# Sixty constant products ahead of the last batch's first tokens, and a change of halves between ScalarE and VectorE

## The chip, the core and the metric

The kernel runs on one core of a Trainium2 chip. The metric is the device time of one execution in microseconds (us), lower is better; the number compared is the median of several runs. The profile is one execution, taken by the hardware profiler, with times from the start of its span.

## What is computed

Attention with a memory term, then a mixture of experts that sends each token to one expert. Cut to what matters here:

```python
B, H, S, D = 4, 8, 576, 64                      # attention
scores = where(causal, -1e9, q @ k.T / sqrt(D))
local = softmax(scores) @ v
out = g * mem_out + (1 - g) * local             # g per head, mem_out from phi(q), M_prev, z_prev
x = out.transpose(0, 2, 1, 3).reshape(2304, 512)

logits = x @ w_gate + modality_bias[modality_id]    # 8 experts
e = argmax(logits); gate_w = softmax(logits)[e]
out[n] = gate_w[n] * (relu(x[n] @ w1[e]) @ w2[e])   # w1 512x1024, w2 1024x512 per expert
```

## The kernel before, in words

Everything is float32; a product of two float32 matrices is made of three faster ones, from a high part and the rest of each operand ("h" and "l" in the names of tiles).

**Order.** A planner (`Plan`) takes every operation with an engine, a planned length, the keys that it reads and writes (`r`, `w`) and a priority, simulates the engines and writes the instructions out in the order in which its simulation starts them. Each engine runs its own list in order. The keys and the planned lengths only set this order. What an engine waits for on the chip is decided afterwards, from the tiles that each instruction really reads and writes.

**Attention** fills the first 310 us or so, head by head. `av` multiplies the probabilities by `vhl`, whose 128 columns are 64 of the high part of v and 64 of its rest, so that a PSUM bank holds the result of the high part on partitions 0 to 63 and that of the rest on 64 to 127. The two have to be added. For half of the heads (`d % 4 < 2`) ScalarE copies both and GpSimd adds them; for the others ScalarE copies one to the tile `avt` (L738) and VectorE adds the other from PSUM (L740), into partitions 0 to 63 of `ot` for an even head and 64 to 127 for an odd one. Each such head has two copies and two additions (128 and 448 columns), 32 of each in all.

**Experts.** After each batch of 576 tokens the gate and `route` write tables of token numbers by expert, and a slot of 256 rows of the fullest expert is worked on at once: `fetch` loads the slot's rows of the tables (SyncE, L1009), `merge` turns them into the tile `ids` (VectorE, L999 and L1000), and GpSimd gathers the tokens from `x_dram` into `xg` (L1016). `slot` then transposes them on TensorE (L1042), ScalarE and VectorE make `xh` and `xl` (L1050, L1052), and TensorE makes 8 groups of 12 products with w1 (L1064), one PSUM bank for each group; ScalarE (relu, L1073, `hh`) and VectorE (the rest, L1075, `hlo`) empty each bank. Products with w2 follow (L1086), 24 for each tile of tokens. Slots 0 to 2 belong to the first three batches. Slot 3 (two tiles of 128 tokens) and slot 4 (two of 96) are the first that can hold tokens of the last batch. All TensorE's results share 8 banks (`pa_90` to `pa_97`). Meanwhile the weights of the second expert are loaded (SyncE, L978) into a ring of four tiles `raw`, rounded by ScalarE (L985) and the rest taken by VectorE (L989), which frees the ring's tile; its last eight pieces are `w2h` and `w2l`.

At the program's start TensorE multiplies a tile of ones by itself 90 times (`warm`, L501).

Of the kernel before, what the change touches and what calls it, by code (L numbers as in the profile page):

```python
# [12 lines left out]
AF = mybir.ActivationFunctionType  # L13
ALU = mybir.AluOpType
# [198 lines left out]
def kernel(  # L213
# [15 lines left out]
    nc = tc.nc  # L229
# [4 lines left out]
    P = 128  # L234
# [13 lines left out]
    EARLY = 3  # L248
# [35 lines left out]
    NH = B * H  # L284
    NAVP = 2
    NRELU = 4
    INPLACE = (0,)
    NWARM = 90
    VHI = "POOL"
    WLO = "POOL"  # L290
    NDBL = 0
# [205 lines left out]
    def warm():  # L497

        t = Slot()
        for i in range(NWARM):  # L500
            g.op("PE", 56, lambda: nc.tensor.matmul(t.ap[:, 0:P], lhsT=ones, rhs=ones, start=True, stop=True),  # L501
                 r=[t] if i else ["ones"], w=[] if i else [t], alloc=None if i else t, prio=("warm", 9))

    def load_t(nm, src, p, prio):
        b, h0 = divmod(p * 2, H)
# [201 lines left out]
    def av(d, prio):  # L707
        p, hh = divmod(d, 2)
        vt = vhl[p % 2]
        ta, tb = Slot(), Slot()  # L710

        def e(src, first, part):
            for kb in range(NB):
                if kb == 0 and part == 0:
                    nc.tensor.matmul(ta.ap[:, 0:P], lhsT=vt[:, 0, hh], rhs=src[:, PTO[0]:PTO[0] + P],
                                     start=first, stop=not first)
                if part == 1:
                    q0 = max(P, kb * P)
                    s0 = PTO[kb] + q0 - kb * P
                    nc.tensor.matmul(tb.ap[:, q0 - P:S - P], lhsT=vt[:, kb, hh], rhs=src[:, s0:s0 + S - q0],  # L720
                                     start=(first and kb == 0), stop=(not first and kb == NB - 1))

        vk = [(x, p % 2, c) for x in ("vh", "vl") for c in (0, 4)]
        for part, (t, du, ky) in enumerate(((ta, 155, "AB"), (tb, 780, "ABCD"))):
            g.op("PE", du, lambda part=part: e(pth[0], True, part), r=vk + [("ph_", 0, x) for x in ky], w=[t], alloc=t,
                 prio=prio, act=0.88)
            g.op("PE", du, lambda part=part: e(ptl[0], False, part), r=vk + [("pl_", 0, x) for x in ky], w=[t], prio=prio,
                 act=0.88)
        o_, a_ = ot[p % 2][64 * hh:64 * hh + 64], avt[0][64 * hh:64 * hh + 64]
        for part, (t, a, z) in enumerate(((ta, 0, P), (tb, P, S))):  # L730
            n, ko = z - a, ("ot", p % 2, hh, part)
            if d % 4 < NAVP:
                g.op("ACT", act_ns(n), lambda t=t, a=a, z=z, n=n: nc.scalar.activation(
                    out=o_[:, a:z], in_=t.ap[0:64, 0:n], func=AF.Copy), r=[t], w=[ko], prio=prio)
                g.op("ACT", act_ns(n), lambda t=t, a=a, z=z, n=n: nc.scalar.activation(  # L735
                    out=a_[:, a:z], in_=t.ap[64:P, 0:n], func=AF.Copy), r=[t], w=[("avt", part)], prio=prio)
            else:
                g.op("ACT", act_ns(n), lambda t=t, a=a, z=z, n=n: nc.scalar.activation(  # L738
                    out=avt[0][0:64, a:z], in_=t.ap[64:P, 0:n], func=AF.Copy), r=[t], w=[("avt", part)], prio=prio)
                g.op("DVE", dve_ns(n), lambda t=t, a=a, z=z, n=n: nc.vector.tensor_tensor(  # L740
                    out=o_[:, a:z], in0=t.ap[0:64, 0:n], in1=avt[0][0:64, a:z], op=ALU.add),
                     r=[t, ("avt", part)], w=[ko], prio=prio)
        if d % 4 < NAVP:
            g.op("POOL", 1420, lambda: nc.gpsimd.tensor_tensor(out=o_, in0=o_, in1=a_, op=ALU.add),
                 r=[("avt", 0), ("avt", 1)], w=[("ot", p % 2, hh, 0), ("ot", p % 2, hh, 1)], prio=prio)
# [286 lines left out]
    def slot(g, u, w, nt, prio, m=P):  # L1032

        i4, i2, n_ = u % 4, pick(u), nt * m
        id_, nc_ = ids[i4], 2 if nt < 3 else 1
        for y in range(KC // nc_):
            ps_ = Slot()

            def e1(y=y, ps_=ps_):
                for c in range(nc_):  # L1040
                    for t in range(nt):
                        nc.tensor.transpose(ps_.ap[:, c * n_ + t * m:c * n_ + (t + 1) * m],  # L1042
                                            xg[i2][0:m, t, (nc_ * y + c) * P:(nc_ * y + c + 1) * P], ident[0:m, 0:m])

            def pv(ps_=ps_):
                return ps_.ap[:, 0:nc_ * n_].rearrange("p (c n) -> p c n", n=n_)

            cs = slice(nc_ * y, nc_ * y + nc_)
            g.op("PE", 107 * nt * nc_, e1, r=[("xg", i2, t) for t in range(nt)], w=[ps_], alloc=ps_, prio=prio)
            g.op("ACT", act_ns(nc_ * n_), lambda cs=cs, pv=pv: nc.scalar.activation(  # L1050
                out=xh[i2][:, cs, 0:n_], in_=pv(), func=AF.Copy), r=[ps_], w=[("xh", i2, nc_ * y // 2)], prio=prio)
            g.op("DVE", dve_ns(nc_ * n_), lambda cs=cs, pv=pv: nc.vector.tensor_tensor(  # L1052
                out=xl[i2][:, cs, 0:n_], in0=pv(), in1=xh[i2][:, cs, 0:n_].bitcast(F32), op=ALU.subtract),
                 r=[ps_, ("xh", i2, nc_ * y // 2)], w=[("xl", i2, nc_ * y // 2)], prio=prio)
        xk = [(x, i2, y) for x in ("xh", "xl") for y in range(2)]
        for f in range(KF):
            hp = Slot()

            def e2(f=f, hp=hp):
                n = 0  # L1060
                w1h, w1l = wt[w][0:2]
                for c in range(KC):
                    for a, x_ in ((w1h, xh[i2]), (w1h, xl[i2]), (w1l, xh[i2])):
                        nc.tensor.matmul(hp.ap[:, 0:n_], lhsT=a[:, c, f * P:(f + 1) * P], rhs=x_[:, c, 0:n_],  # L1064
                                         start=(n == 0), stop=(n == 3 * KC - 1))
                        n += 1

            g.op("PE", 12 * pe_ns(n_) + 25, e2, r=xk + [k_ for c in range(KC) for k_ in wkeys(w, c)],
                 w=[hp], alloc=hp, prio=prio)
            for i, (a, z) in enumerate(((0, min(n_, 2 * P)), (2 * P, n_))):  # L1070
                if a >= z:
                    continue
                g.op("ACT", act_ns(z - a), lambda f=f, hp=hp, i=i, a=a, z=z: nc.scalar.activation(  # L1073
                    out=hh[i][:, f, 0:z - a], in_=hp.ap[:, a:z], func=AF.Relu), r=[hp], w=[("hh", i, f)], prio=prio)
                g.op("DVE", dve_ns(z - a), lambda f=f, hp=hp, i=i, a=a, z=z: nc.vector.scalar_tensor_tensor(  # L1075
                    out=hlo[i][:, f, 0:z - a], in0=hp.ap[:, a:z], scalar=0.0, in1=hh[i][:, f, 0:z - a].bitcast(F32),
                    op0=ALU.max, op1=ALU.subtract), r=[hp, ("hh", i, f)], w=[("hl", i, f)], prio=prio)
        for t in range(nt):
            op, hi, ts = Slot(), t // 2, slice(t % 2 * m, (t % 2 + 1) * m)
            for y in range(4):  # L1080
                def e3(y=y, op=op, hi=hi, ts=ts):
                    n = 0
                    w2h, w2l = wt[w][2:4]
                    for f in range(2 * y, 2 * y + 2):
                        for a, w_ in ((hh[hi], w2h), (hh[hi], w2l), (hlo[hi], w2h)):
                            nc.tensor.matmul(op.ap[0:m], lhsT=a[:, f, ts], rhs=w_[:, f],  # L1086
                                             start=(y == 0 and n == 0), stop=(y == 3 and n == 5))
                            n += 1

                g.op("PE", 6 * pe_ns(512), e3, r=[(x, hi, f) for x in ("hh", "hl") for f in range(2 * y, 2 * y + 2)] +  # L1090
                     wkeys(w, KC + y), w=[op], alloc=op if y == 0 else None, prio=prio)
            oi = 0 if u < EARLY else next_osb()
            g.op("ACT", act_ns(512, True, 1), lambda t=t, op=op, oi=oi: nc.scalar.activation(  # L1093
                out=osb[oi][0:m], in_=op.ap[0:m], func=AF.Copy, scale=id_[0:m, t, 1:2].bitcast(F32)),
                 r=[op, ("ids", i4)], w=[("osb", oi)], prio=prio)
            store(u, t, m, oi, prio)
# [228 lines left out]
    o = 0  # L1325
    for x, (nt, m) in enumerate(NST0):
        fetch(g, u, start(EARLY, o), nt, ["swap"], ("f1", NH + 2 * x), m=m)
        slot(g, u, 0, nt, ("e1", NH + 2 * x), m=m)
        o += nt * m
        u += 1  # L1330
# [91 lines left out]
```

## Time and profile before

| | us |
|---|---|
| time, median of 3 runs (lowest, highest) | 551.55 (549.52, 552.14) |
| profiled execution, its own time | 550.81 |
| its span, first to last instruction | 549.1 |
| TensorE (PE) busy | 497.9, 91% |
| VectorE (DVE) busy | 330.5, 60% |
| ScalarE (ACT) busy | 329.0, 60% |
| GpSimd (POOL) busy | 251.9, 46% |

[...] Shares are means over the whole span; attention and the experts have different limits, and the stretch around the change is read by itself below.

### The profile page before, as it was taken

The page shows a single profiled execution, that of the slowest core. Times are in us where ns is not written, and L with a number is a line of the kernel's source. Part 1 is how long each engine was busy: PE and PEld are TensorE (multiplying, and loading weights), DVE is VectorE, ACT ScalarE, POOL GpSimd, SP SyncE. Part 2 cuts the span into 40 slices and gives each one's busy share as a digit, 9 for nine tenths or more (in the row PEclk, how much of TensorE's full clock was granted, in tenths as well). Part 3 has the DMA queues.
Part 4 walks back from the last instruction along what each step waited for, and adds up shares of the span by engine and source line. Part 5 has one row for each costly group of instructions (what it writes and reads, how often), then busy time and mean ns, then how long its engine had stood idle before and what let it go on. Part 6 is the DMA issues. An engine that isn't in the chain of part 4 may idle for free. (4 is left out here: it accounts for less than half of the span.)

```text
span 549.1 us, 10861 instructions
## 1 busy us (share of the span) xinstructions
PE 497.9 (91%) x3420; PEld 445.1 (81%) x3420; DVE 330.5 (60%) x1066; ACT 329.0 (60%) x923; POOL 251.9 (46%) x257
## 2 busy tenths in 40 slices
PE   8898899987899889979898999769999999999992
PEld 8787888875787778869897898769897987989891
DVE  3788788897798988988878336653315512313010
ACT  4798898986999979979298244333325513222110
POOL 8462984656788768865761062350030004010100
PEclk9799899999899989989899999979999999999997
DMA  5888887988777997953740025474036203000100
GB/s 96 189 206 169 206 201 182 231 189 154 192 176 198 238 189 191 220 164 95 180 110 3 20 61 180 78 233 146 18 96 182 83 19 88 29 19 21 40 0 36
DMA packets 97101, 70.43 MB, mean 128 GB/s; under 512 B 73936, under 2 KB 74320, under 8 KB 97042
## 3 DMA queue, kind: packets, MB, share of 16 engines
q1 hardware_dynamic: 93330, 59.99, 45.2%
q0 software_dynamic: 3712, 9.72, 5.8%
q8 instruction: 28, 0.46, 0.4%
q14 instruction: 31, 0.25, 0.2%
HBM read 32.36 MB, written 10.16 MB: 77 GB/s over the span
## 5 line engine op out<-in xcount | busy, mean ns | idle before, releaser
L675 ACT ACTIVATE P<-P,nm 128x576 f32<-128x576 f32 (+4 forms) x160 | 88.5, 558 | 9.1 <-DVE nm L669 6.0
L1024 POOL DMA_INDIRECT out_dram<-osb,ids x19 | 18.9, 997 | 156.0 <-ACT osb L1093 115.3
L1064 PE MATMUL pa<-xh,w1h 128*128 128x256 f32 (+2 forms) x288 | 84.4, 293 | 2.6 <-ACT xh L1050 2.6
L1064 PE MATMUL pa<-xl,w1h 128*128 128x256 f32 (+2 forms) x288 | 83.4, 290 | 0.5 <-DVE xl L1052 0.3
L1064 PE MATMUL pa<-xh,w1l 128*128 128x256 f32 (+2 forms) x288 | 83.1, 288 | 0.0
L1075 DVE SCALAR_TENSOR_TENSOR hlo<-pa,hh 128x256 fp32r<-128x256 f32 (+1 forms) x72 | 29.8, 416 | 69.8 <-ACT hh L1073 69.7
L703 DVE TENSOR_TENSOR ptl<-pa,pth 128x512 fp32r<-128x512 f32 (+1 forms) x128 | 65.6, 564 | 3.0 <-ACT pth L701 2.4
L1073 ACT ACTIVATE hh<-pa 128x256 fp32r<-128x256 f32 (+1 forms) x80 | 29.0, 367 | 61.1 <-PE pa L1064 54.2
L669 DVE CUSTOM_DVE_ANT_0 P<-pa,maskw 128x320 f32<-128x320 f32 (+3 forms) x160 | 62.2, 427 | 4.2 <-PE pa L657 3.5
L684 PE MATMUL pa<-ident,P 128*128 128x128 f32 x320 | 57.6, 285 | 4.0 <-ACT P L675 3.7
L657 PE MATMUL pa<-ks,qs 128*128 128x192 f32 (+3 forms) x186 | 55.5, 329 | 5.9 <-ACT avt L735 2.9
L1086 PE MATMUL pa<-w2h,hh 128*128 128x512 f32 (+1 forms) x152 | 60.4, 397 | 0.0
L701 ACT ACTIVATE pth<-pa 128x512 fp32r<-128x512 f32 (+1 forms) x128 | 57.0, 511 | 5.0 <-PE pa L684 4.4
L1086 PE MATMUL pa<-w2l,hh 128*128 128x512 f32 (+1 forms) x152 | 59.6, 392 | 0.0
L1064 PEld LDWEIGHTS pa<-xh,w1h 128*128 128x128 f32 x288 | 55.6, 193 | 3.4 <-ACT xh L1050 2.9
L1064 PEld LDWEIGHTS pa<-xl,w1h 128*128 128x128 f32 x288 | 55.6, 193 | 1.2 <-DVE xl L1052 0.9
L1086 PE MATMUL pa<-w2h,hlo 128*128 128x512 f32 (+1 forms) x144 | 56.5, 392 | 0.0
L1064 PEld LDWEIGHTS pa<-xh,w1l 128*128 128x128 f32 x288 | 55.5, 193 | 0.0
L1093 ACT ACTIVATE osb<-pa,ids 128x512 f32<-128x512 f32 (+1 forms) x19 | 13.1, 687 | 68.4 <-PE pa L1086 63.1
L657 PE MATMUL pa<-kls,qs 128*128 128x192 f32 (+3 forms) x186 | 49.2, 295 | 0.4 <-DMA kls<-kl 0.4
L684 PEld LDWEIGHTS pa<-ident,P 128*128 128x128 f32 x320 | 40.4, 147 | 6.3 <-ACT P L675 6.0
L684 PE MATMUL pa<-swp,P 128*128 128x128 f32 x160 | 39.5, 287 | 6.1 <-DVE kl L617 2.5
(234 smaller groups left out, 1198.9 us busy)
## 6 DMA issues: line engine op xcount, KB each, us to landing
ks<-kh SPq DMA_DIRECT2D x62, 144.0 KB, 3.0
kls<-kl SPq DMA_DIRECT2D x62, 144.0 KB, 3.4
raw<-in_moe_w_dram SPq DMA_DIRECT2D x32, 256.0 KB, 3.5
qn<-in_q_dram SPq DMA_DIRECT2D x32, 144.0 KB, 4.3
kn<-in_k_dram SPq DMA_DIRECT2D x32, 144.0 KB, 4.2
qs<-qh SPq DMA_DIRECT2D x31, 144.0 KB, 2.6
qs<-ql SPq DMA_DIRECT2D x31, 144.0 KB, 2.7
vn<-in_v_dram SPq DMA_DIRECT2D x32, 128.0 KB, 3.0
```

The source lines that it names most:

```text
L657: nc.tensor.matmul(t.ap[0:m, o:o + z - x], lhsT=l[:, QS[j]:QE[j]], rhs=r[:, x:z], start=(i == 0), stop=(i == len(terms) - 1))
L669: nc.vector.tensor_tensor_reduce(out=pj[:, x:z], in0=t.ap[0:m, o:o + z - x], in1=mk, scale=-1.0, scalar=nm if x else 3.0e38, op0=ALU.add, ...
L675: g.op("ACT", act_ns(w, False, 2), lambda pj=pj, nm=nm, den=den, w=w: nc.scalar.activation(out=pj[:, 0:w], in_=pj[:, 0:w], func=AF.Exp, sc ...
L684: nc.tensor.transpose(t[:, o:o + P], prow[c % NPB][j][:, kb * P:(kb + 1) * P], swp if j == kb else ident)
L701: g.op("ACT", act_ns(n), lambda t=t, o=o, n=n: nc.scalar.activation(out=hi[:, o:o + n], in_=t.ap[:, 0:n], func=AF.Copy), r=[t], w=[("ph_", ...
L703: g.op("DVE", dve_ns(n), lambda t=t, o=o, n=n: nc.vector.tensor_tensor(out=lo[:, o:o + n], in0=t.ap[:, 0:n], in1=hi[:, o:o + n].bitcast(F3 ...
L1024: g.op("POOL", 1310, lambda: nc.gpsimd.indirect_dma_start(out=out[:, :], out_offset=bass.IndirectOffsetOnAxis(ap=ids[u % 4][0:m, t, 0:1].b ...
L1064: nc.tensor.matmul(hp.ap[:, 0:n_], lhsT=a[:, c, f * P:(f + 1) * P], rhs=x_[:, c, 0:n_], start=(n == 0), stop=(n == 3 * KC - 1))
L1073: g.op("ACT", act_ns(z - a), lambda f=f, hp=hp, i=i, a=a, z=z: nc.scalar.activation(out=hh[i][:, f, 0:z - a], in_=hp.ap[:, a:z], func=AF.R ...
L1075: g.op("DVE", dve_ns(z - a), lambda f=f, hp=hp, i=i, a=a, z=z: nc.vector.scalar_tensor_tensor(out=hlo[i][:, f, 0:z - a], in0=hp.ap[:, a:z] ...
L1086: nc.tensor.matmul(op.ap[0:m], lhsT=a[:, f, ts], rhs=w_[:, f], start=(y == 0 and n == 0), stop=(y == 3 and n == 5))
L1093: g.op("ACT", act_ns(512, True, 1), lambda t=t, op=op, oi=oi: nc.scalar.activation(out=osb[oi][0:m], in_=op.ap[0:m], func=AF.Copy, scale=i ...
```

## The change

Two things. `hot` puts 60 products of the tile of ones into the plan, keyed to the `ids` of slot 3 and ahead of slot 3's transposes. And in `av`, for the heads that VectorE adds, ScalarE now copies partitions 0 to 63 of the bank, and VectorE reads partitions 64 to 127 of the bank beside partitions 0 to 63 of `avt`.

```diff
+    NHOT = 60
+    def hot(u):
+        t = Slot()
+        for i in range(NHOT):
+            g.op("PE", 56, lambda: nc.tensor.matmul(t.ap[:, 0:P], lhsT=ones, rhs=ones, start=True, stop=True),
+                 r=[t] if i else [("ids", u % 4)], w=([] if i else [t]) + ["hot"] * (i == NHOT - 1), alloc=None if i else t,
+                 prio=("f1", NH))
...
-                    out=avt[0][0:64, a:z], in_=t.ap[64:P, 0:n], func=AF.Copy), r=[t], w=[("avt", part)], prio=prio)
+                    out=avt[0][0:64, a:z], in_=t.ap[0:64, 0:n], func=AF.Copy), r=[t], w=[("avt", part)], prio=prio)
-                    out=o_[:, a:z], in0=t.ap[0:64, 0:n], in1=avt[0][0:64, a:z], op=ALU.add),
+                    out=o_[:, a:z], in0=t.ap[64:P, 0:n], in1=avt[0][0:64, a:z], op=ALU.add),
...
-            g.op("PE", 107 * nt * nc_, e1, r=[("xg", i2, t) for t in range(nt)], w=[ps_], alloc=ps_, prio=prio)
+            g.op("PE", 107 * nt * nc_, e1, r=[("xg", i2, t) for t in range(nt)] + (["hot"] if u == EARLY else []), w=[ps_], alloc=ps_, prio=prio)
...
         fetch(g, u, start(EARLY, o), nt, ["swap"], ("f1", NH + 2 * x), m=m)
+        if x == 0:
+            hot(u)
         slot(g, u, 0, nt, ("e1", NH + 2 * x), m=m)
```

Up to the products the order of all engines is the same as before; GpSimd's and SyncE's stay the same to the end. The lines of the changed kernel stand 9 higher in this part (L1064 is L1073 there, L1042 is L1051, L1086 is L1095, L989 is L998, L1075 is L1084, L1052 is L1061).

TensorE before, from the end of slot 2's seventh group. The tile `xh_109` is slot 2's, `xg_4300` and `xh_4296` are slot 3's, `xg_108` is slot 4's; what an instruction waits for stands in brackets.

```order
L1064 MATMUL pa_96<-xh_109,w1l_99 128x256
L1042 MATMUL pa_93<-ident,xg_4300 128x128 [waits DMAHW5_49,DMAHW6_49,DMASW6_49,PE_49]
L1042 MATMUL pa_93<-ident,xg_4300 128x128 [waits DMASW7_49]
...
L1064 MATMUL pa_94<-xh_109,w1h_98 128x256 [waits DVE_49]
...
L1086 MATMUL pa_95<-w2h_100,hh_111 128x512 [waits DVE_49]
...
L1064 MATMUL pa_91<-xh_4296,w1h_98 128x256 [waits DVE_49,Activation_49]
```

After it come five groups of slot 3, the transposes of slot 4, and 18 more products with w2. TensorE in the changed kernel, from the end of slot 2's third group:

```order
L1073 MATMUL pa_95<-xh_109,w1l_99 128x256
L509 LDWEIGHTS ones
L509 MATMUL pa_91<-ones 128x128
...
L1051 MATMUL pa_96<-ident,xg_4300 128x128 [waits DMAHW5_49,DMAHW6_49,DMASW6_49,PE_49]
...
L1073 MATMUL pa_92<-xh_109,w1h_98 128x256 [waits DVE_49]
...
L1051 MATMUL pa_94<-ident,xg_108 128x96 [waits DMASW0_49,DVE_49]
...
L1073 MATMUL pa_91<-xh_4296,w1h_98 128x256 [waits Activation_49]
...
L1095 MATMUL pa_93<-w2h_100,hh_111 128x512 [waits DVE_49]
```

The 60 products stand behind slot 2's third group, with no wait in front of them; its groups 4 and 5 follow, then slot 3's transposes, group 6, slot 4's transposes, four groups of slot 3, groups 7 and 8 of slot 2 (into `pa_93` and `pa_92`), 12 products with w2 into `pa_93`, slot 3's fifth group, 12 more products with w2, and slot 3's sixth group. Before, slot 2's groups 1 to 7 all stood ahead of slot 3's transposes.

VectorE before, from slot 3's `xl` to slot 4's:

```order
L1052 TENSOR_TENSOR xl_4297<-pa_93,xh_4296 128x2x256
L1052 TENSOR_TENSOR xl_4297<-pa_92,xh_4296 128x2x256
L989 TENSOR_TENSOR w2l_4295<-raw_4306,w2h_4294 128x512
L1075 SCALAR_TENSOR_TENSOR hlo_112<-pa_94,hh_111 128x256
L989 TENSOR_TENSOR w2l_4295<-raw_4307,w2h_4294 128x512
L989 TENSOR_TENSOR w2l_4295<-raw_4304,w2h_4294 128x512
L989 TENSOR_TENSOR w2l_4295<-raw_4305,w2h_4294 128x512
L989 TENSOR_TENSOR w2l_4295<-raw_4306,w2h_4294 128x512
L989 TENSOR_TENSOR w2l_4295<-raw_4307,w2h_4294 128x512
L1052 TENSOR_TENSOR xl_110<-pa_92,xh_109 128x2x192
```

VectorE in the changed kernel, the same stretch:

```order
L1061 TENSOR_TENSOR xl_4297<-pa_96,xh_4296 128x2x256
L1061 TENSOR_TENSOR xl_4297<-pa_93,xh_4296 128x2x256
L1084 SCALAR_TENSOR_TENSOR hlo_112<-pa_92,hh_111 128x256
L998 TENSOR_TENSOR w2l_4295<-raw_4307,w2h_4294 128x512
L998 TENSOR_TENSOR w2l_4295<-raw_4304,w2h_4294 128x512
L998 TENSOR_TENSOR w2l_4295<-raw_4305,w2h_4294 128x512
L998 TENSOR_TENSOR w2l_4295<-raw_4306,w2h_4294 128x512
L998 TENSOR_TENSOR w2l_4295<-raw_4307,w2h_4294 128x512
L1084 SCALAR_TENSOR_TENSOR hlo_112<-pa_93,hh_111 128x256
L1084 SCALAR_TENSOR_TENSOR hlo_112<-pa_92,hh_111 128x256
L1061 TENSOR_TENSOR xl_110<-pa_94,xh_109 128x2x192
```

The `hlo` of slot 2's groups 7 and 8 (`pa_93`, `pa_92`) now stand behind the last five pieces of w2. On ScalarE the two relus moved in the same way, behind the last five pieces of `w2h`.

## Rows read from the trace of the kernel before

**Rows 1.** The page's part 2: TensorE's busy tenths in 40 slices of 13.7 us.

```profile
PE   8898899987899889979898999769999999999992
```

**Rows 2.** TensorE by time: start, length, instructions; in brackets idle time before and its releaser.

```profile
353.16 0.28 PE L1064 MATMUL pa<-xh,w1l 128*128 128x256 f32 x1
...
358.60 0.28 PE L1064 MATMUL pa<-xh,w1l 128*128 128x256 f32 x1
362.13 0.45 PE L1042 MATMUL pa<-ident,xg 128*128 128x128 f32 x1 [3.25 <-issue]
364.03 1.75 PE L1042 MATMUL pa<-ident,xg 128*128 128x128 f32 x7 [1.46 <-DMA xg<-x_dram,ids]
365.44 0.56 PE L1064 MATMUL pa<-xh,w1h 128*128 128x256 f32 x1
...
368.14 0.41 PE L1086 MATMUL pa<-w2h,hh 128*128 128x512 f32 x1
...
369.56 0.28 PE L1064 MATMUL pa<-xh,w1h 128*128 128x256 f32 x1
...
376.63 0.82 PE L1042 MATMUL pa<-ident,xg 96*128 96x96 f32 x8
...
377.55 0.40 PE L1086 MATMUL pa<-w2l,hh 128*128 128x512 f32 x1
...
381.52 0.28 PE L1064 MATMUL pa<-xh,w1h 128*128 128x256 f32 x1
```

**Rows 3.** Stretches of 1 us: engines' busy time, then granted clock, DMA share, GB/s.

```profile
361.00:362.00 1.00, 0.00 (x0) 0.00 (x0) 0.83 (x2) 0.95 (x3) 0.70 (x2) 0.66 0.75 146
...
368.00:369.00 1.00, 1.00 (x6) 0.86 (x6) 0.28 (x2) 0.39 (x1) 0.15 (x1) 0.92 0.86 260
```

**Rows 4.** TensorE at the program's start, by time: the products of ones.

```profile
7.95 1.84 PE L501 MATMUL pa<-ones 128*128 128x128 bf16 x30
9.72 0.35 PE L657 MATMUL pa<-kh,qh 64*128 64x192 f32 x1
```

**Rows 5.** By time: VectorE's merge for slot 3, last gathers of slots 3 and 4.

```profile
356.89 0.15 DVE L1000 TENSOR_REDUCE ids<-idr 128x2 f32<-128x6 f32 x1
...
359.20 1.07 POOL L1016 DMA_INDIRECT xg<-x_dram,ids  x1 [0.31 <-issue]
...
361.88 1.36 POOL L1016 DMA_INDIRECT xg<-x_dram,ids  x1 [0.30 <-issue]
```

**Rows 6.** The last piece of w2 on ScalarE and VectorE, and slot 2's last `hlo`.

```profile
375.74 0.63 ACT L985 ACTIVATE w2h<-raw 128x512 fp32r<-128x512 f32 x1 [1.74 <-DMA raw<-in_moe_w_dram]
...
376.41 0.69 DVE L989 TENSOR_TENSOR w2l<-raw,w2h 128x512 fp32r<-128x512 f32 x1 [1.68 <-ACT w2h L985]
...
368.77 0.42 DVE L1075 SCALAR_TENSOR_TENSOR hlo<-pa,hh 128x256 fp32r<-128x256 f32 x1 [0.72 <-ACT hh L1073]
```

**Rows 7.** VectorE around an addition of an even head, then of an odd one.

```profile
149.34 0.46 DVE L617 TENSOR_TENSOR kl<-pa,kh 128x288 fp32r<-128x288 f32 x1
149.72 0.27 DVE L740 TENSOR_TENSOR ot<-pa,avt 64x128 f32<-64x128 f32 x1
149.92 0.44 DVE L617 TENSOR_TENSOR kl<-pa,kh 128x288 fp32r<-128x288 f32 x1
...
154.96 0.08 DVE L669 DVE_READ_ACCUMULATOR2_ANT nm<- 64x1 f32 x1
155.07 0.28 DVE L740 TENSOR_TENSOR ot<-pa,avt 64x128 f32<-64x128 f32 x1
155.39 0.62 DVE L669 CUSTOM_DVE_ANT_0 P<-pa,maskw 128x448 f32<-128x448 f32 x1
```

**Rows 8.** ScalarE's copies of 448 columns, by form: busy, mean ns, idle before.

```profile
L738 ACT ACTIVATE avt<-pa 64x448 f32<-64x448 f32 x16 | 8.6, 538 | 2.2 <-PE pa L720 2.0
L733 ACT ACTIVATE ot<-pa 64x448 f32<-64x448 f32 x16 | 8.6, 536 | 3.4 <-PE pa L720 3.2
```

**Rows 9.** Sum of three stretches of attention, 20 to 300 us: busy by engine.

```profile
sum 280.00, PE 250.18 PEld 223.96 DVE 236.44 ACT 241.77 POOL 188.85; mean PE 83.39 PEld 74.65 DVE 78.81 ACT 80.59 POOL 62.95
```

## The prediction

> **What bounds the kernel now.** I read the page's slices first: the emptiest slice of TensorE behind the start is the 27th, 357 to 371 us (a 6), and from there on every slice but the last is a 9 [rows 1]. So time lost before 371 is not given back later. Then TensorE by time in and around that slice, and the clock in stretches of 1 us. Slot 2's groups run without a gap until 358.71 (the last product starts at 358.60, and they stand 0.113 us apart: 48 steps from 353.16); one transpose of slot 3 runs at 362.13, after 3.25 us idle, when the first gathered tile is there, and the other seven from 364.03, after 1.46 us idle for the gather, when the second is [rows 2]. That is a hole of 5.3 us with one transpose in it. Inside it the granted clock falls to half: it is 0.66 over the microsecond from 361, so it fell at about 361.3, and 0.92 over that from 368, so it rose at about 368.2 [rows 3]. [...] What this costs is in the rows: the seven transposes take 1.41 us (364.03 to 365.44), where eight are 0.82 long at 376.63, and slot 2's eighth group takes 2.70 (365.44 to 368.14) for twelve products that take 1.36 at 0.113 each [rows 2]. So the hole costs 5.2 us of waiting and some 2.0 us of slow work. From slot 3's sixth group on, at 381.52, TensorE's order is the same before and after; what is lost there is lost at the end.
>
> **The products.** In the plan they wait for slot 3's `ids`. In the program they wait for nothing: they read only the ones and write a free bank, and no wait stands in front of them in the order. So they start right behind the third group, at 353.16 + 0.11 = 353.3. One costs 0.059 us (30 from 7.95 to 9.72) [rows 4], or twice that at the lower level of the clock. TensorE has the higher one here (0.113 for 256 columns, which took 0.225 at the lower), so I take the first: 60 x 0.059 = 3.5 us, end at 356.8. Groups 4 and 5 of slot 2 (24 x 0.113 = 2.7) end at 359.5. The tokens still come at 364.03, for GpSimd's and SyncE's lists are unchanged, and VectorE's merges stand behind no group that moved. So the hole is still there, 4.5 instead of 5.3 us long, only shifted; what fills it ran ahead of it. The products' own time is covered by this hole (with 0.118 each they end at 360.4 and the groups at 363.1, still before 364.03); without that cover they would cost 3.5 to 7.1 us.
>
> **What moved behind the hole.** Before, seven groups of slot 2 stood ahead of slot 3's transposes; now five. Two groups, 2 x 1.36 = 2.7 us, move from a place with spare time to one with none. I count on from 364.03 with the clock low as before: transposes to 365.44, group 6 to 368.14, slot 4's transposes (0.8; the last gather of slot 3, issued at 359.20, was there 4.8 us later, so slot 4's, issued at 361.88, should be by about 367 [rows 5]) to 368.9, four groups of slot 3 at 1.41 (five from 369.56 to 376.63 [rows 2]) to 374.6, groups 7 and 8 to 377.3.
>
> **The new wait.** Next on TensorE are 12 products with w2 into `pa_93`, the bank of group 7. They must wait until VectorE's `hlo` has emptied it, and that now stands behind the last piece of `w2l`, as its relu stands behind the last `w2h`. That piece's time is set by a load: ScalarE waited 1.74 us for it and began at 375.74, VectorE at 376.41 for 0.69 [rows 6]. Nothing that moved delays or hastens this chain, since the loads are issued by SyncE, whose list is unchanged, and wait for ring tiles that earlier pieces free. So `hlo` runs from 377.1 for 0.42 us and TensorE starts at 377.5: a wait of 0.2 us behind its own arrival at 377.3. Queued behind it are slot 3's fifth group and everything after. Then 12 products at 0.2335 (17 from 377.55 to 381.52), 2.8; one group, 1.4; 12 more, 2.8: slot 3's sixth group starts at 384.5. Before it was 381.52. The difference is **+3.0 us**.
>
> Bounds of this term: the bank keeps it from being less than +3.0 as long as the last piece comes when it did. The slow stretch can reach further. If one as long as before (6.9 us, 361.3 to 368.2) began only at 364.0, it would reach to 370.9: 2.7 us more at half speed, 1.4 us lost, of which 0.2 are in the wait already, so +4.2. I take +3.0, since the hole ends where it did.
>
> **The halves.** ScalarE's copies cost the same from either half: 538 ns from the upper (L738), 536 from the lower (L733) [rows 8]. That part is nothing. VectorE's additions: an even head's (all operands on partitions 0 to 63) starts at 149.72, 0.08 before the instruction ahead ends, and the next starts 0.07 before its end. An odd head's, whose result alone lies on the upper half, starts 0.03 after the end of the one ahead (155.04), and the next 0.04 after its end (155.35) [rows 7]. Changing the half costs 0.11 us on either side. After the change all 32 additions read the upper half of PSUM. The trace has no addition that changes the half of an input only, so the bounds are: nothing, if only the result's half counts (16 of 32 as now); or 16 x 0.22 = 3.5 us of VectorE's time, if the input's counts as well. VectorE is not the engine that TensorE always waits for: from 20 to 300 us TensorE is idle 280 - 250.2 = 29.8 us, 10.7% [rows 9]. I take 3.5 x 0.107 = **0.4 us**, near the lower end, because delays of a tenth are mostly taken up by other waits. There is nothing to gain here. [...]
>
> **Sum.** The profiled execution took 550.81; 550.81 + 3.0 + 0.4 = 554.2. The median of the runs is 0.74 above it, so against the median: 551.55 + 3.4 = **555.0**. A change below 0.5% (2.8 us, 548.8 to 554.3) can hardly be told from none here: the three runs already span 2.6 us.
>
> **Rivals.**
> - *The products do wait for `ids`.* The merge for slot 3 ends at 357.04 [rows 5]. TensorE would stand from 353.3 to 357.1, the products end at 360.6, groups 4 and 5 at 363.3, still before 364.03: the same end, 555.0. Against it: no wait in the order. Chance 0.06.
> - [...] Chance 0.11. [...]
> - *VectorE's holds all reach the end:* 3.0 + 3.5 = 6.5, 558.1. For it: VectorE is 84% busy in attention (236.4 of 280 us). Against: TensorE's idle share. Chance 0.12.
> - *Something unseen in attention* (the clock also falls there, and a shift of a tenth can move that): faster than 548.8, chance 0.04.
>
> **How the numbers follow.** My forecast, products without a wait, the hole kept, 3 to 4.2 us lost and up to 1 in attention, has 0.67: 555.0. The range goes from the case of the kept clock, 552.5, to the holds, 558.0. Slower than 554.3: three quarters of the forecast and of the first rival (0.57), all of the third (0.12), together 0.69. Faster 0.04. The rest, 0.27, is within 0.5%.
>
> **What the profile will show.** If I am right: 60 products of ones starting right behind a group, before the merge for slot 3; after groups 4 and 5 a wait of 4 to 5 us at L1051 for the gather; the granted clock at half for some microseconds behind it; a short wait of L1095 for VectorE's `hlo`; slot 3's sixth group 3 us later, counted from the gather. VectorE's additions of even heads starting after the end of the instruction ahead would show the input's half to count. I am wrong if the products fill the hole itself, if the last `w2h` comes well before its place now, or if TensorE has new idle time in attention of more than a microsecond or two.

## The result and the profile after

| | median, us (lowest to highest) | executions |
|---|---|---|
| before | 550.53 (547.97 to 552.14) | 4 |
| changed | 557.55 (552.85 to 559.07) | 4 |

The ratio is 1.014, with an interval of 1.0092 to 1.0188: slower by 7.0 us (5 to 10 by the interval), where 3.4 were forecast; the time lies inside the range. Ratios here leave out the longest executions of a kernel and medians don't, so the two can differ a little. The profiled execution of the changed kernel is its shortest, 552.85 us, with a span of 551.1.

The page's part 2, TensorE's busy tenths in 40 slices, answers to [rows 1]:

```profile
PE   8799899997899889889889999869999999999992
```

The hole is in the same slice, the 27th, and behind it are again only 9s. TensorE by time in that stretch, which answers to [rows 2] (start, length, instructions, idle time before and its releaser):

```profile
352.05 0.28 PE L1073 MATMUL pa<-xh,w1l 128*128 128x256 f32 x1
352.17 3.52 PE L509 MATMUL pa<-ones 128*128 128x128 bf16 x60
...
358.30 0.28 PE L1073 MATMUL pa<-xh,w1l 128*128 128x256 f32 x1
359.57 0.30 PE L1051 MATMUL pa<-ident,xg 128*128 128x128 f32 x1 [1.00 <-issue]
361.04 0.98 PE L1051 MATMUL pa<-ident,xg 128*128 128x128 f32 x7 [1.17 <-DMA xg<-x_dram,ids]
361.78 0.36 PE L1073 MATMUL pa<-xh,w1h 128*128 128x256 f32 x1
...
363.39 0.27 PE L1051 MATMUL pa<-ident,xg 96*128 96x96 f32 x1
365.51 0.80 PE L1051 MATMUL pa<-ident,xg 96*128 96x96 f32 x7 [1.85 <-DMA xg<-x_dram,ids]
...
366.82 0.58 PE L1073 MATMUL pa<-xl,w1h 128*128 128x256 f32 x1 [0.37 <-DVE xl L1061]
...
376.65 0.40 PE L1095 MATMUL pa<-w2h,hh 128*128 128x512 f32 x1
...
383.67 0.28 PE L1073 MATMUL pa<-xh,w1h 128*128 128x256 f32 x1
```

VectorE by time, its merge for slot 3, which answers to [rows 5]:

```profile
354.63 0.15 DVE L1009 TENSOR_REDUCE ids<-idr 128x2 f32<-128x6 f32 x1
```

The products start at 352.17 behind a group, 2.5 us before this merge, so they wait for no `ids`. From slot 3's second token tile (361.04) to its sixth group (383.67) TensorE now takes 22.6 us; before it was 17.5. The first new wait is at slot 4's second token tile, 1.85 us, on which I had not counted. The seven transposes run at full speed (0.74 us from 361.04 to 361.78, granted clock 1.00), so the clock did not fall in the hole. It fell later, as the stretches of 1 us show (engines' busy time, granted clock, DMA share, GB/s); they answer to [rows 3]:

```profile
362.00:363.00 1.00, 1.00 (x11) 1.00 (x10) 0.38 (x2) 0.00 (x0) 0.75 (x1) 1.00 1.00 351
...
366.00:367.00 1.00, 0.63 (x6) 0.43 (x5) 1.00 (x3) 0.69 (x2) 0.00 (x0) 0.73 0.89 314
367.00:368.00 1.00, 1.00 (x5) 1.00 (x6) 0.70 (x2) 0.00 (x0) 0.00 (x0) 0.50 0.95 268
```

VectorE around an addition of 128 columns and one of 448, both of even heads, beside [rows 7]:

```profile
148.81 0.46 DVE L626 TENSOR_TENSOR kl<-pa,kh 128x288 fp32r<-128x288 f32 x1
149.30 0.29 DVE L749 TENSOR_TENSOR ot<-pa,avt 64x128 f32<-64x128 f32 x1
149.63 0.46 DVE L626 TENSOR_TENSOR kl<-pa,kh 128x288 fp32r<-128x288 f32 x1
150.12 0.63 DVE L749 TENSOR_TENSOR ot<-pa,avt 64x448 f32<-64x448 f32 x1
150.66 0.15 DVE L778 SCALAR_TENSOR_TENSOR rnm<-mt,gg 128x10 f32<-128x10 f32 x1
```

The addition at 149.30 starts 0.03 us after the end of the instruction ahead (before: 0.08 ahead of it), and the next one starts 0.04 after its end (before: 0.07 ahead of it). So in these rows the half of an input counts, 0.11 us on either side; I call these later starts holds. The instruction at 150.66, which reads nothing from PSUM, starts 0.09 before the end at 150.75. What the holds cost is another matter. Sum of the same three stretches of attention, 20 to 300 us, which answers to [rows 9]:

```profile
sum 280.00, PE 249.91 PEld 223.78 DVE 237.60 ACT 239.04 POOL 188.14; mean PE 83.30 PEld 74.59 DVE 79.20 ACT 79.68 POOL 62.71
```

TensorE is idle 30.1 us there, 0.3 more than before.

### The profile page after: what moved, and what is told of

Same layout as the page of the kernel before. It is cut to its first block, busy times and chain, and to the rows that moved or that the text cites. A ratio compares the mean times of both kernels' runs of the same rounds, so it can differ in the third digit from the quotient of the medians.

```text
span 551.1 us, 10981 instructions
## 1 busy us (share of the span) xinstructions
PE 499.9 (91%) x3480; PEld 446.7 (81%) x3480; DVE 331.3 (60%) x1066; ACT 325.1 (59%) x923; POOL 252.3 (46%) x257
## 5 line engine op out<-in xcount | busy, mean ns | idle before, releaser
L1073 PE MATMUL pa<-xh,w1h 128*128 128x256 f32 (+2 forms) x288 | 84.7, 294 | 2.7 <-ACT xh L1059 2.7
L1073 PE MATMUL pa<-xl,w1h 128*128 128x256 f32 (+2 forms) x288 | 84.0, 292 | 0.6 <-DVE xl L1061 0.4
L1073 PE MATMUL pa<-xh,w1l 128*128 128x256 f32 (+2 forms) x288 | 83.5, 290 | 0.0
L1084 DVE SCALAR_TENSOR_TENSOR hlo<-pa,hh 128x256 fp32r<-128x256 f32 (+1 forms) x72 | 29.8, 416 | 71.8 <-ACT hh L1082 71.6
L1095 PE MATMUL pa<-w2h,hh 128*128 128x512 f32 (+1 forms) x152 | 60.3, 397 | 0.0
L1095 PE MATMUL pa<-w2l,hh 128*128 128x512 f32 (+1 forms) x152 | 59.6, 392 | 0.0
L693 PE MATMUL pa<-ident,P 128*128 128x128 f32 x320 | 56.2, 280 | 3.7 <-ACT P L684 3.5
L1073 PEld LDWEIGHTS pa<-xh,w1h 128*128 128x128 f32 x288 | 55.8, 194 | 3.5 <-ACT xh L1059 3.0
L1073 PEld LDWEIGHTS pa<-xl,w1h 128*128 128x128 f32 x288 | 55.9, 194 | 1.6 <-DVE xl L1061 1.3
L1095 PE MATMUL pa<-w2h,hlo 128*128 128x512 f32 (+1 forms) x144 | 56.5, 392 | 0.0
L1073 PEld LDWEIGHTS pa<-xh,w1l 128*128 128x128 f32 x288 | 55.9, 194 | 0.0
```

What stands on the lines that cost most here:

```text
L693: nc.tensor.transpose(t[:, o:o + P], prow[c % NPB][j][:, kb * P:(kb + 1) * P], swp if j == kb else ident)
```

## The experiments

All ratios are against runs of the kernel before on the same chip. In short:

| | median, us (executions) | before | ratio, 95% |
|---|---|---|---|
| products only | 553.56 (12) | 548.05 (33) | 1.0118 [1.0078, 1.0157] |
| halves only | 550.17 (12) | 548.05 (33) | 0.9977 [0.9936, 1.0018] |
| order only | 552.63 (10) | 548.05 (33) | 1.0075 [1.0040, 1.0109] |
| 60 in the hole, order of before | 549.01 (12) | 548.05 (33) | 1.0023 [0.9990, 1.0056] |
| changed, again | 554.58 (6) | 548.99 (23) | 1.0112 [1.0073, 1.0151] |
| 60 early, order of before | 550.31 (12) | 548.99 (23) | 1.0015 [0.9982, 1.0047] |
| 30 in the hole | 547.83 (12) | 548.99 (23) | 0.9992 [0.9957, 1.0026] |
| 40 ahead of slot 2's groups | 550.09 (12) | 548.64 (29) | 1.0014 [0.9976, 1.0053] |
| the same 40, and the planned 60 | 553.81 (12) | 548.64 (29) | 1.0069 [1.0030, 1.0108] |
| 40, and 30 in the hole | 549.66 (12) | 548.64 (29) | 0.9980 [0.9944, 1.0016] |

**Each part alone.** First the products without the change of halves (the two lines of `av` as before):

> The products with their place in the plan, without the change of halves. If the order around slot 3 makes the loss (my first term): +3.0 us, ratio 1.005, and slot 3's sixth group about 3 us later counted from slot 3's last gather. If the halves make most of it: within 0.3% of before, since what is left here is covered by the hole. If the whole 7 us belong to the products (more low clock, or a longer hole than the first term holds): ratio 1.010 or more.

It came out 1.0118, which is 4.3 to 8.6 us by its interval: as much as the whole change, as far as can be told. TensorE by time at slot 3's second token tile, for which it still waited, and at the first product with w2 into the bank of group 7, which `hlo` did hold, as the forecast had it:

```profile
363.26 0.98 PE L1051 MATMUL pa<-ident,xg 128*128 128x128 f32 x7 [1.53 <-DMA xg<-x_dram,ids]
...
377.12 0.50 PE L1095 MATMUL pa<-w2h,hh 128*128 128x512 f32 x1 [0.47 <-DVE hlo L1084]
```

Then the halves alone, in the kernel before:

```diff
-                    out=avt[0][0:64, a:z], in_=t.ap[64:P, 0:n], func=AF.Copy), r=[t], w=[("avt", part)], prio=prio)
+                    out=avt[0][0:64, a:z], in_=t.ap[0:64, 0:n], func=AF.Copy), r=[t], w=[("avt", part)], prio=prio)
...
-                    out=o_[:, a:z], in0=t.ap[0:64, 0:n], in1=avt[0][0:64, a:z], op=ALU.add),
+                    out=o_[:, a:z], in0=t.ap[64:P, 0:n], in1=avt[0][0:64, a:z], op=ALU.add),
```

> The change of halves alone; the order of all engines is that of before. As I predicted it: +0.4 us, no difference that can be told (ratio 1.001). If the holds of VectorE's additions reach the end in full: +3.5 us or a little more, ratio 1.006 to 1.008, and the even heads' additions start 0.03 us after the end of the instruction ahead instead of 0.08 before it. If the holds shift attention so that the granted clock is low more often: more than 3.5 us, with a lower mean granted clock than before in the same call.

No difference that can be told: 0.9977, with bounds of -3.5 and +1.0 us. So by these bounds VectorE's holds don't reach the end in full. The third case of the expectation stays open: the mean granted clock was 0.965 over these 12 executions against 0.970 over the 33 of before, which is not clear of their spread, and the medians differ by 2.1 us the other way.

**The order without the products.** They stay in the plan and are not issued (the lines of `av` as before); everything else keeps the changed order:

```diff
-            g.op("PE", 56, lambda: nc.tensor.matmul(t.ap[:, 0:P], lhsT=ones, rhs=ones, start=True, stop=True),
+            g.op("PE", 56, lambda: None,
```

> The plan with the 60 products, halves as before, but the products are not issued: the order of every engine is that of the changed kernel without them. If the moved groups and the wait for the bank make the loss, the 3.5 us of products are covered and this is as slow as the products alone: +2.5 to +3.0 us, ratio 1.005. If the products themselves cost (they delay groups 4 and 5 past the gather), this is 2 to 3.5 us faster than the products alone, near 1.000.

1.0075: the order alone costs 4.1 us (2.2 to 6.0 by its interval). In its trace TensorE does slot 3's transposes with the clock low (0.50 from 365 to 371 us, 1.76 for seven), and slot 4's right behind them without a wait:

```profile
363.48 0.30 PE L1051 MATMUL pa<-ident,xg 128*128 128x128 f32 x1 [4.22 <-issue]
365.99 1.76 PE L1051 MATMUL pa<-ident,xg 128*128 128x128 f32 x7 [2.21 <-DMA xg<-x_dram,ids]
...
370.10 1.30 PE L1051 MATMUL pa<-ident,xg 96*128 96x96 f32 x8
...
386.77 0.28 PE L1073 MATMUL pa<-xh,w1h 128*128 128x256 f32 x1
```

From 365.99 to 386.77 are 20.8 us; I had worked out 20.5.

**Products without the order.** Order of before, and 60 products right in front of slot 3's first transpose, so that they run ahead of its wait for the first token tile:

```diff
+                if u == EARLY and y == 0:
+                    for _ in range(NHOT):
+                        nc.tensor.matmul(ps_.ap[:, 0:P], lhsT=ones, rhs=ones, start=True, stop=True)
```

> Before's order and halves, with 60 products of ones put right ahead of slot 3's first transpose, so that they run in the hole before its gather lands. If the clock stays high because of them: the granted clock is 1.00 from the products to slot 3, the transposes and the next group run at 0.113 a product, 1.5 to 2.0 us faster, ratio 0.997. If the clock falls anyway, or the products end behind the gather: 0 to +1 us, ratio 1.000 to 1.002.

1.0023, not to be told from before. TensorE by time:

```profile
359.82 1.51 PE L1043 MATMUL pa<-ones 128*128 128x128 bf16 x24
361.83 0.27 PE L1043 MATMUL pa<-ones 128*128 128x128 bf16 x2 [0.49 <-issue]
362.58 2.06 PE L1043 MATMUL pa<-ones 128*128 128x128 bf16 x34 [0.48 <-issue]
364.48 1.04 PE L1046 MATMUL pa<-ident,xg 128*128 128x128 f32 x8
```

TensorE never stands for more than 0.49 us here and the transposes run at full speed (eight in 1.04 us, granted clock 1.00), yet nothing is gained: the products end at 364.48, and the transposes begin that late. The gather of slot 3's second tile was issued at 358.06, 6.4 us earlier; by the estimate made for the early products below, the tokens had been there for about 0.9 to 2.3 us. With 30 of them (`NHOT` 30):

> As the 60 products right ahead of slot 3's first transpose, but 30. If the 60 gained nothing because they run past the gather (they ended at the moment the transposes began), 30 end 1.8 us earlier and keep the clock up: ratio 0.996 to 0.999. If the clock then falls as without them: 1.000.

0.9992, no gain that can be told either (-2.4 to +1.4 us). In its trace the 30 end when the transposes begin, 4.55 us behind that issue (358.34 to 362.89), about when the tokens come, and the sixth group follows 16.0 us later. And the 60 behind slot 2's third group, where the change has them, but with groups 4 to 7 still ahead of the transposes:

```diff
+                if u == EARLY - 1 and f == 3:
+                    for _ in range(NHOT):
+                        nc.tensor.matmul(hp.ap[:, 0:P], lhsT=ones, rhs=ones, start=True, stop=True)
```

> Before's order and halves, with the 60 products issued behind slot 2's third group and all its groups 4 to 7 still ahead of slot 3's transposes. If the hole covers them, as I predicted: within 0.2% of before, and the groups end about when the gather lands or ahead of it. If the hole is often shorter than the 3.5 us of products, as the trace of the halves alone (2.0 us) says: +1 to +2.5 us, ratio 1.002 to 1.005.

1.0015. So 60 products in the old order cost at most 2.6 us, by the upper end of this interval. In its trace the hole is gone: the last group's product is followed at once by eight transposes, and between the groups stands a stop that the profile gives to nothing:

```profile
366.45 0.28 PE L1068 MATMUL pa<-xl,w1h 128*128 128x256 f32 x1 [0.72 <-issue]
...
368.35 0.28 PE L1068 MATMUL pa<-xh,w1l 128*128 128x256 f32 x1
368.46 1.04 PE L1043 MATMUL pa<-ident,xg 128*128 128x128 f32 x8
```

GpSimd's gather of slot 3's second tile, by time, in the same trace:

```profile
362.11 1.01 POOL L1017 DMA_INDIRECT xg<-x_dram,ids  x1 [0.31 <-issue]
```

The transposes begin 6.35 us after this issue. Where TensorE stood and waited for that tile, it came 4.1 us (changed kernel, profiled execution) to 5.5 us (order only) after the issue. So here the tokens had been there for about 0.8 to 2.2 us, an estimate, and not the gather but TensorE's own work set the start: the products, and slot 2's groups, which ran with the granted clock at 0.50 from 351 to 357 us in this trace.

**The changed kernel again,** unaltered, for a second trace and more executions:

> The changed kernel as it is, with more executions. If its loss is the products' order alone (products alone 553.6 against 548.05, +5.5): ratio 1.009 to 1.011. If the halves add the 1 to 2 us that their medians showed: 1.012 to 1.014. In the trace, from the start of slot 3's seven transposes to its sixth group: 20.5 us by my sum (17.5 before); 21 to 23 if the wait for slot 4's tokens comes on top.

1.0112. TensorE by time:

```profile
355.73 3.52 PE L509 MATMUL pa<-ones 128*128 128x128 bf16 x60
...
361.49 0.28 PE L1073 MATMUL pa<-xh,w1h 128*128 128x256 f32 x1 [0.23 <-issue]
362.24 0.28 PE L1073 MATMUL pa<-xh,w1l 128*128 128x256 f32 x1 [0.34 <-issue]
362.96 0.28 PE L1073 MATMUL pa<-xl,w1h 128*128 128x256 f32 x1 [0.32 <-issue]
...
363.44 0.28 PE L1073 MATMUL pa<-xh,w1l 128*128 128x256 f32 x1
363.56 1.03 PE L1051 MATMUL pa<-ident,xg 128*128 128x128 f32 x8
...
366.47 0.80 PE L1051 MATMUL pa<-ident,xg 96*128 96x96 f32 x7 [0.38 <-DMA xg<-x_dram,ids]
...
368.23 0.39 PE L1073 MATMUL pa<-xl,w1h 128*128 128x256 f32 x1 [0.66 <-issue]
...
384.00 0.28 PE L1073 MATMUL pa<-xh,w1h 128*128 128x256 f32 x1
```

Here the hole is used up to the last: groups 4 and 5 end at 363.56, and the transposes follow without a wait. The granted clock is 1.00 from 354 us on, and still 20.4 us pass from 363.56 to the sixth group.

**The kernel before, twice more,** one execution each:

> The kernel before once more, for a second trace. If the hole ahead of slot 3's transposes is a fixed 5 us: 5 us again from the end of slot 2's seventh group to the seven transposes. If it depends on the clock during slot 2's groups: 2 to 4 us where the clock is low in them.

> The kernel before for a third trace. If the first trace was the rarer case: the clock low in slot 2's groups and a hole of 2 to 3 us. If the second was: a hole of 5 us and the clock low behind it.

The first took 545.09 us. TensorE by time:

```profile
357.72 0.28 PE L1064 MATMUL pa<-xh,w1l 128*128 128x256 f32 x1
358.47 0.30 PE L1042 MATMUL pa<-ident,xg 128*128 128x128 f32 x1 [0.47 <-issue]
360.17 0.98 PE L1042 MATMUL pa<-ident,xg 128*128 128x128 f32 x7 [1.40 <-DMA xg<-x_dram,ids]
360.91 0.36 PE L1064 MATMUL pa<-xh,w1h 128*128 128x256 f32 x1
...
375.76 0.28 PE L1064 MATMUL pa<-xh,w1h 128*128 128x256 f32 x1
```

and its stretches of 2 us, the granted clock third from the right:

```profile
348.00:350.00 2.00, 2.00 (x13) 2.00 (x13) 1.29 (x7) 0.90 (x2) 0.00 (x0) 0.61 0.26 96
360.00:362.00 2.00, 1.83 (x16) 1.83 (x17) 1.04 (x5) 0.91 (x3) 0.60 (x1) 1.00 1.03 289
```

The second took 548.85:

```profile
357.44 0.28 PE L1064 MATMUL pa<-xh,w1l 128*128 128x256 f32 x1
359.93 0.30 PE L1042 MATMUL pa<-ident,xg 128*128 128x128 f32 x1 [2.21 <-PE pa L1064]
361.46 1.75 PE L1042 MATMUL pa<-ident,xg 128*128 128x128 f32 x7 [1.23 <-DMA xg<-x_dram,ids]
...
379.58 0.28 PE L1064 MATMUL pa<-xh,w1h 128*128 128x256 f32 x1
```

The hole is 2.3 us in the first (357.84 to 360.17) and 3.9 in the second (357.56 to 361.46), where the execution that I worked from had 5.3. In the first the clock was low in slot 2's groups, 0.61 from 348 to 350 us (TensorE had stood 2.28 us ahead of them for `xh`; in the execution that I worked from it stood there for 2.62 and the clock stayed at 1.00), and then was not low behind the hole: its seven transposes take 0.74 us, and the sixth group follows 15.6 us after the tokens, where it was 17.5 in [rows 2] and 18.1 in the second.

**The clock in slot 2's groups held up.** 40 products between slot 2's transposes and its first group, in the order of before:

```diff
+                if u == EARLY - 1 and f == 0:
+                    for _ in range(40):
+                        nc.tensor.matmul(hp.ap[:, 0:P], lhsT=ones, rhs=ones, start=True, stop=True)
```

> Before's order and halves, with 40 products of ones between slot 2's transposes and its first group, where TensorE waits 2.3 us for xh. If the clock falls in that wait in most executions and so sets the length of the later hole: the granted clock is 1.00 through slot 2's groups, the hole is 4 us or more, the clock falls behind it, and the time stays within 0.3% of before (what the groups gain, the hole takes). If the hole is set by something else: it stays at 2 us.

then with the planned 60 and their order as well:

> The planned 60 products (halves as before) together with the 40 that keep the clock up in slot 2's groups. If the size of the hole is what my sum got wrong, the loss against the kernel with the 40 alone is the +3.0 of my sum (the profile it was made from had the clock up there): ratio to before 1.005 to 1.007. If the loss has another cause: 1.010 or more, as with the products alone.

and with 30 in the hole instead:

> Before's order and halves with both the 40 products at slot 2's wait and 30 in the hole ahead of slot 3's transposes, so that the clock could stay up from slot 2 to slot 4. If the gather's landing bounds this stretch: 15.6 us from slot 3's seven transposes to its sixth group, as in the second trace of before, and 0 to 1 us gained, ratio 0.998 to 1.000. If TensorE's work bounds it: 2 to 3 us gained, ratio 0.995.

1.0014, 1.0069 and 0.9980. By these ratios the second is 3.0 us slower than the first, with a standard error of 0.9: what was expected if the sum had gone wrong by the size of the hole. In the trace of the first the clock is at 1.00 in slot 2's groups, the hole is 4.7 us (360.07 to 364.81) and the clock is low behind it, 0.50 from 364 to 370 us. In the trace of the second, too, the clock is low behind the hole (0.50 from 365 to 367 us), and the way from slot 3's tokens to its sixth group is 20.5 us (364.67 to 385.17):

```profile
364.67 1.76 PE L1051 MATMUL pa<-ident,xg 128*128 128x128 f32 x7 [1.26 <-DMA xg<-x_dram,ids]
...
385.17 0.28 PE L1076 MATMUL pa<-xh,w1h 128*128 128x256 f32 x1
```

In the trace of the third the 30 products did not keep the clock up: it is at 0.50 from 362 to 368 us, and the seven transposes run at half speed.

```profile
357.96 1.85 PE L1043 MATMUL pa<-ones 128*128 128x128 bf16 x30
...
362.65 1.75 PE L1046 MATMUL pa<-ident,xg 128*128 128x128 f32 x7 [1.35 <-DMA xg<-x_dram,ids]
```

None of the three can be told to beat the kernel before.

## Why the forecast had the sign right and half the size

**What held.** The products wait for nothing, and run behind the third group ahead of the merge. The order is the main cost: alone it gives 1.0075, and without it the same products give 1.0015 and 1.0023. With the clock low behind the hole, the forecast's case, the way from slot 3's tokens to its sixth group is what was worked out, 20.5: 20.8 with the order only, 20.5 with the 40 and 60. From that sixth group on all traces are alike, as forecast: 167.6 us to the end of the span in the one I worked from (381.52 to 549.1), 167.4 after (383.67 to 551.1).

**What did not hold beside it.** The wait of 4 to 5 us for the gather was 1.00 and 1.17 us, and the clock did not fall there but later, at about 366.5. The bank's wait was 0.47 us with the products only, and in the first trace of the changed kernel there was none (376.65). In the recorded chances, three quarters of 0.67 and 0.06 are 0.55, not 0.57. That the time lay inside the range is luck in part: the 551.55 that it was added to, from three executions, lies above the medians of the 85 later ones of before (548.05 to 548.99).

**The step that failed** is the order's term: "The difference is **+3.0 us**", with "I take +3.0, since the hole ends where it did". It counts from the 17.5 us that one execution took from slot 3's second token tile to its sixth group, with the clock low, as the kernel's own, and it lets slot 4's tokens be there without a wait. The term measured +4.1 with the order alone (548.05 x 0.0075). That way in the traces, in us:

```
order of before   17.5 (worked from), 15.6 and 18.1 (again), 17.2 (halves only)        mean 17.1
changed order     22.6 and 20.4 (changed), 21.0 (products only), 20.8 (order only)     mean 21.2
```

The starts not shown above are 365.27 and 382.42 (halves only) and 384.24 (products only). The means differ by 4.1 as well. They rest on four traces each, and the interval of the order alone, 2.2 to 6.0, holds 3.0 too. The rest of the miss is open: the whole change measured 7.0, and 6.2 the second time (4.0 to 8.3), some 2 to 3 more than the order. The traces don't place it. Behind the sixth group they are alike, and ahead of it they scatter anyway: slot 2's first transpose starts between 342.3 and 347.5 us, with no rule by kernel. The clock also falls in attention: in these eight traces and that of the 40 and 60 it is below 0.9 in 20 to 35 of the first 340 stretches of 1 us.

*The order.* Where the clock stays high, the kernel before needs 15.6 us from the tokens to the sixth group, 1.9 less than I counted from. The changed kernel can't use that. With the clock high throughout it still takes 20.4 (363.56 to 384.00), and 21.0 with the products only (363.26 to 384.24): two groups more stand in the way (2 x 1.41 = 2.8), and TensorE, arriving sooner, meets waits that a low clock hides (1.85 us for slot 4's second tile in the first trace, none in that of the order only). Slot 4's transposes now stand behind one group instead of six, and their second tile comes only at 366.47, 2.9 us after the transposes' start in that trace and 4.5 after it in the first one (361.04 to 365.51). I had it "there by about 367" and TensorE at 368.1, because I ran it at half speed. So by single traces the price is about 3.0 when the clock is low in both, and 20.4 - 15.6 = 4.8 when it is high in both. The runs with the 40 products fit: where those keep the clock up in slot 2's groups, the traces with and without the 60 have a long hole and a low clock behind it, the forecast's case, and the planned 60 with their order cost 3.0 us, with a standard error of 0.9. The recorded range puts the case of a kept clock at its lower end, 552.5. No run shows this term: in the traces a kept clock makes the price higher, since the kernel before gains by it (15.6 instead of 17.5 and 18.1) and the changed kernel's order does not (20.4 and 21.0 instead of 20.8 and 20.5). What the kernel before gains I had not asked.

*The products.* "The products' own time is covered by this hole" held where a trace can show it: behind the products and the groups TensorE still waited for slot 3's second tile in the first trace of the changed kernel (1.17), with the products only (1.53) and with the 40 and 60 (1.26). Nor did they delay its gather, which GpSimd issues 12.7 to 14.7 us behind the start of slot 2's first transpose in all traces, with products or without. But the cover of 5.3 us that I priced them under was 3.9 and 2.3 in the other two traces of before, and the products and their stops used it to the last in the second trace of the changed kernel (transposes at 363.56). An execution with a short hole can pay for them; how much that adds to the time is not shown. Sorted by the mean granted clock of an execution, since times follow it (about 2.6 us for each 0.01 over 78 executions of before), the means are (us, number of executions):

```
granted clock     before        order only   products only   changed
0.955 to 0.965    550.32 (24)   554.33 (5)   556.43 (3)      557.35 (4)
0.965 to 0.975    548.33 (34)   551.95 (4)   552.41 (7)      554.41 (6)
```

At like clock the order costs 3.6 to 4.0, the products 0.5 to 2.1 more, and the whole change 6.1 to 7.0. The numbers in the rows are small. 1.0118 against 1.0075 points to the products as well, but the intervals overlap, and the plain means of the executions behind these two ratios are 0.5 us apart, with a standard error of 1.0. Nor is it settled why the clock falls in some executions ahead of slot 2's groups and in others behind them.

**The halves.** Of my two bounds for VectorE's time the upper one is right about the holds, 0.11 us on either side for even heads too, and the trace of before could not say so. That delays of a tenth are mostly taken up by other waits was my estimate; 0.4 us for the whole was near enough to what can be told, since the measured bounds hold both it and 0, and not the 3.5 of the rival. The last column above is 0.9 to 2.0 over the one beside it, which these few executions don't separate from 0.4.

**The clock as a gain.** In [rows 2] and [rows 3] the clock fell while TensorE stood, at about 361.3, 2.6 us behind the last product, and rose while it worked, at about 368.2, 4.2 us after the seven transposes began. In the changed kernel it fell at about 366.5, 1 us after TensorE had begun again behind its wait of 1.85. That constant products can buy the clock here is not shown. It stayed at 1.00 with 60 and with 30 of them in the hole, but it was 1.00 when they began; it stayed at 1.00 in one trace of before with none (360.17); and it fell to 0.50 at about 362 behind the 30 that followed the 40. No version gained time that can be told: 60 products end later than the tokens come, and what 30 might save, about 1 us (16.0 against the mean of 17.1), is within the bounds of that run.

## What to carry to other kernels

Spare time read from one trace is a sample: look at the same gap in several executions before pricing work under it as free. When an order moves work, work the sum out at both levels of the clock (1.00 and 0.50 here), for the kernel before as well as for the changed one, and ask at each which load or gather the engine then meets first. A key that only a planner knows delays nothing on the chip (the products started 2.5 us ahead of the merge that they were keyed to): filler meant for a wait must stand in the engine's own list right in front of the instruction that waits, and it has to end before what is waited for comes; 60 products, 4.7 us long with their stops, did not here.

## What the runs showed of the hardware

The mean granted clock of one and the same program differs from execution to execution, and its time with it: the kernel before took 543.1 to 553.3 us at 0.956 to 0.982 (78 executions), about 2.6 us for each 0.01 by a straight line through them. TensorE also stops for 0.23 to 0.72 us at a time inside and behind a train of 60 small products, with no releaser in the profile ("issue"): two stops of 0.49 and 0.48 among the 60 in the hole, one of 0.72 in the groups behind them in the old order, three of 0.23 to 0.34 in one of the two traces of the changed kernel and none in the other. Slot 2's groups in the three traces of the kernel before have none. What causes them is not known.
